# Two weight tiles of the dense mixture begin in the attention's wide score banks, one step before the fourth pair's values

## The chip, the cores and the metric

The kernel runs on one core of one Trainium2 chip. The metric is the device time of one execution in microseconds (us), the median of several runs. Engines are named as in the profile: PE is TensorE's matmul side and PEld its weight load, DVE is VectorE, ACT ScalarE, POOL GpSimd, and SP the engine whose queue issues the transfers.

## The reference, cut to what matters

Three stages follow one another. Only the first two meet at the place of the change.

```python
# 1. attention, B=4, H=8, S=576, D=64, block mask of 64
scores = where(block_i >= block_j, q @ k.T / sqrt(D), -1e9)
attn = softmax(scores);  x = (attn @ v)        # -> x: 2304 tokens x 512
# 2. dense mixture: w1, w2, w3 are 512 x 768, w_out is 768 x 512
h = maximum(maximum(x @ w1, x @ w2), x @ w3);  x = h @ w_out
# 3. four experts, weighted by normalised domain_probs
out = sum_e p[:, e] * (relu(x @ w1[e]) @ w2[e])
```

## The kernel before

**Attention by pairs of heads.** There are 16 pairs, `n` from 0 to 15, four to a batch. A turn of the main loop finishes pair `n` and starts pair `n + 1`. Its steps stand in a list, `todo`. `scores(n + 1, 0)`, `(…, 1)` and `(…, 2)` (steps s0, s1, s2) multiply q by k into PSUM (L181, L202), DVE takes the row minimum (L218), ACT the exponential (L225), and a later `normalise` multiplies by the reciprocal of the sum (POOL L251 from pair 4 on; for pairs 0 to 3 the output is scaled in `weigh` instead). `turn_probs` transposes probabilities on PE (L279), and ACT and DVE copy them out (L289): ta[0], ta[1] are the first part for either head, tb[0], tb[1] the second. `values(n)` (step va, L314) multiplies by v. For batch 0, `weigh` (transposes L337 and L341, products L342 and L345) scales the result. `prep_pair` (step pp) prepares the pair after the next.

**PSUM.** Eight banks: `ps_x` has four one-bank buffers (tag x) that scores, transposes and `weigh` take in turn. `ps_c` is one buffer of two banks (tag c), in which only step s2 of the first eight pairs puts part of its scores (and the last step of later pairs). `ps_v` has two banks for the values of batch 0. When batch 0's attention is over, `ps_v` is closed, and its banks become `ps_m`, two one-bank buffers for the mixture. From pair 4 on a run of scores begins only when all the buffers it needs are free (`whole`, with the ends kept in `x_ends` and `c_ends`).

**The mixture as filler.** `moe1(b)` is a generator for batch `b`: for each of six column tiles of h it multiplies three weight tiles (w1, w2, w3), each as 12 matmuls (four pairs' slices `d` of x, times the three terms high-high, high-low, low-high) of 128x128 by 128x512, L480, into one `ps_m` bank. ACT copies the first result to `mt` (L524), DVE takes the maximum with the others (L526). Then come four tiles of w_out. `Filler.upto` draws units of it between attention's steps of the next batch, by a pace: a turn's position `at` gives the units due, less `LAG` = 9. A weight tile of 12 matmuls counts three units. `moe1_inputs(b, ds)` splits the attention's output for pairs `ds` into a high and a low part (ACT L502, DVE L503). It is called for the first three pairs before the seventh step of a batch's last turn, and for the fourth pair after its values.

**Weights.** Before batch 0 uses a weight tile, `Convert` loads it and turns it into two float32 parts (ACT L399, L400, L94; POOL L405, L412; DVE L407, L408, L421), up to five tiles and two wide ones ahead.

**Order.** The program is traced in this order, and a scheduler then orders each engine's instructions by a timeline of its own: an instruction whose operands are ready and whose engine is free may go ahead of others that were traced earlier. On the chip each engine takes its instructions strictly in the order so fixed.

Of the kernel before, what the change touches and what calls it, by code (L numbers as in the profile page):

```python
# [6 lines left out]
F32 = mybir.dt.float32  # L7
# [5 lines left out]
ALU = mybir.AluOpType  # L13
# [8 lines left out]
P = 128  # L22
# [5 lines left out]
def program(tc, q, k, v, w123, w_out, probs, e_w1, e_w2, out):  # L28
    nc = tc.nc
# [5 lines left out]
    KD = DM // P  # L35
    NF = FF // P
    NPAIR = H // 2
# [5 lines left out]
    def f(ap):  # L43
        return ap.bitcast(F32)
# [26 lines left out]
    ps_c = attn.enter_context(tc.tile_pool(name="ps_c", bufs=1, space=PSUM, side="right"))  # L71
# [4 lines left out]
    mp = moe.enter_context(tc.tile_pool(name="moe", bufs=1))  # L76
    MAIN = 512
# [13 lines left out]
    pairs, later, made, exps, normal, least = {}, [], {}, [], [], []  # L91
# [48 lines left out]
    x_ends, c_ends = [], []  # L140
# [190 lines left out]
    def weigh(n, behind):  # L331

        pair = pairs[n]
        with tc.issue_after(behind.ins):
            rt = ps_x.tile([P, 512], F32, name="rt", tag="x")
            for m, i in enumerate((0, 2, 3, 1)):
                nc.tensor.transpose(  # L337
                    rt[:, P * i:P * (i + 1)], pair["rb"][:, m].rearrange("p h c -> p (h c)"), ident
                )
            r4 = pair["pv0"][:, P:2 * P]  # L340
            nc.tensor.transpose(r4, pair["rb4"], ident)  # L341
        x_ends.append([nc.vector.tensor_tensor(pair["xf"][:, 0:512], rt, pair["xf"][:, 0:512], op=ALU.mult)])  # L342
        for h in range(2):
            x = pair["xf"][own[h], 512:S]
            nc.vector.tensor_tensor(x, r4[own[h], 64 * h:64 * h + 64], x, op=ALU.mult)  # L345
# [12 lines left out]
    def weight_tile(n, wide):  # L358
        if wide:
            tag, bufs = "wo", 2  # L360
        else:
            tag, bufs = (("wt", 3), ("wu", WT - 3))[taken[0] % WT >= 3]
            taken[0] += 1
        return mp.tile([P, 2, tiles[n].shape[1], P], F32R, name=tag, tag=tag, bufs=bufs)
# [90 lines left out]
    def moe_weight(b, n):  # L455

        if b == 0:
            wt = convert.weight(n)
        else:
            A = tiles[n].shape[1]  # L460
            if b == B - 1 and n == 0:
                taken[0] = 0
            wide = n >= 3 * NF
            if b == B - 1 and not wide and n % WT >= 3:
                wide = True
                taken[0] += 1
            wt = weight_tile(n, wide)
            nc.sync.dma_start(out=f(wt[:].rearrange("p k a f -> p k (a f)")), in_=held[n][:, :, 0:A * P])
        return wt[:, 0], wt[:, 1]
# [5 lines left out]
    def mm3(out_, terms):  # L475
        n = 3 * len(terms)
        m = 0
        for wh, wl, xh, xl in terms:
            for w, x in ((wh, xh), (wh, xl), (wl, xh)):
                nc.tensor.matmul(out=out_, lhsT=w, rhs=x, start=m == 0, stop=m == n - 1)  # L480
                m += 1
                if m % 4 == 0 and m < n:
                    yield
# [3 lines left out]
    xs = {}  # L487

    def moe1_inputs(b, ds):
        if b not in xs:  # L490
            xs[b] = (
                mp.tile([P, KD, MAIN], F32R, name="xh", tag="xh"),
                mp.tile([P, KD, MAIN], F32R, name="xl", tag="xl"),
            )
        xh, xl = xs[b]
        for d in ds:
            xf = pairs[b * NPAIR + d]["xf"]
            rs = slice(b * REST, (b + 1) * REST)
            for cs, h, l in (
                (slice(0, MAIN), xh[:, d], xl[:, d]), (slice(MAIN, S), rest_x[0][:, d, rs], rest_x[1][:, d, rs]),  # L500
            ):
                nc.scalar.copy(h, xf[:, cs])  # L502
                nc.vector.tensor_tensor(l, xf[:, cs], f(h), op=ALU.subtract)  # L503

    def moe1(b):
        hidden = [mp.tile([P, NF, MAIN], F32R, name=x, tag=x) for x in ("hh", "hl")]
        whole = arena.rearrange("p (b d s) -> p d b s", b=B, d=KD)
        hs = [[x[:, ff] for ff in range(NF)] for x in hidden]
        runs = [(MAIN, "mt", *xs[b], *hs, lambda d: x2f[b][:, d, 0:MAIN])]
        if b == B - 1:  # L510
            room = [rest_h] + [mp.tile([P, 2, 2, B * REST], F32R, name="wu", tag="wu", bufs=2) for _ in range(2)]
            hs = [[x[:, i, j] for x in room for j in range(2)] for i in range(2)]
            runs.append((B * REST, "mr", *rest_x, *hs, lambda d: whole[:, d, :, MAIN:S]))
        for ff in range(NF):
            prev = [None] * len(runs)
            for n in range(3):
                wh, wl = moe_weight(b, 3 * ff + n)
                for c, (w, tag, xh, xl, hh, hl, _) in enumerate(runs):
                    m = ps_m.tile([P, 512], F32, name="m", tag="m")[:, 0:w]
                    yield from mm3(m, [(wh[:, d], wl[:, d], xh[:, d], xl[:, d]) for d in range(KD)])  # L520
                    t = prev[c]
                    if t is None:
                        t = prev[c] = mp.tile([P, w], F32, name=tag, tag=tag, bufs=2)
                        nc.scalar.copy(t, m)  # L524
                    else:
                        nc.vector.tensor_tensor(t, m, t, op=ALU.max)  # L526
                    if n == 2:
                        nc.gpsimd.tensor_scalar(hh[ff], t, 1.0, 0.0, op0=ALU.mult, op1=ALU.add)
                        nc.gpsimd.tensor_tensor(hl[ff], t, f(hh[ff]), op=ALU.subtract)
                    yield  # L530
        for d in range(KD):
            wh, wl = moe_weight(b, 3 * NF + d)
            for w, _, _, _, hh, hl, to in runs:
                m = ps_m.tile([P, 512], F32, name="m", tag="m")[:, 0:w]
                yield from mm3(m, [(wh[:, ff], wl[:, ff], hh[ff], hl[ff]) for ff in range(NF)])
                x = to(d)
                nc.scalar.copy(x, m if len(x.shape) == 2 else m.rearrange("p (b s) -> p b s", b=B))  # L537
                yield

    class Filler:  # L540
        def __init__(self):
# [15 lines left out]
    filler = Filler()  # L557

    def stage(fn, *args):
        old = later[:]  # L560
        later.clear()
        if fn is not None:
            fn(*args)
        for x in old:
            x()
# [16 lines left out]
    for n in range(NALL):  # L582
        b, d = divmod(n, NPAIR)
        ahead = n + 2 < NALL
        prep = prep_pair(n + 2) if ahead else iter(())
        g = 2 * n
        ta, tb = [[(turn_probs, g + h, part) for h in range(2)] for part in range(2)]
        va = (values, n)
        apart = n + 1 < 2 * NPAIR
        s0, s1, s2 = [(scores, n + 1, i) if n + 1 < NALL else (None,) for i in (0, 1 if apart else 3, 2)]  # L590
        pp = (next, prep, None)
        if apart:
            todo = [ta[0], s0, pp, tb[0], s1, ta[1], tb[1], s2, pp, va]
        else:
            todo = [ta[0], s0, pp, tb[0], ta[1], tb[1], s1, pp, va]
        for m, st in enumerate(todo):
            if d == NPAIR - 1 and m == 6:
                moe1_inputs(b, range(KD - 1))
            stage(*st)
            if b == 0 and m == 3 and n:  # L600
                weigh(n - 1, made["pv"])
            if d == NPAIR - 1 and m == len(todo) - 1:
                if b == 0:
                    weigh(n, made["pv"])
                moe1_inputs(b, [KD - 1])
            at = (n + (m + 1) / len(todo)) / NPAIR
            filler.upto((at - 1) * UNITS - LAG)
        if n + 4 < NALL:
            load_pair(n + 4)
        if d == NPAIR - 1:  # L610
            if b == 0:
                first.close()
                ps_m = ps.enter_context(tc.tile_pool(name="ps_m", bufs=2, space=PSUM, reuse_waits="tile"))
            filler.work.append(moe1(b))
# [26 lines left out]
    def tile_of(p, c, t):  # L641
        return (2 * p + c) * TPC + t

    pr = xp.tile([P, NTT, E], F32, name="pr", tag="pr")
    for p in range(NPASS):
        for c in range(2):
            if p < NPASS - 1:
                r0 = (2 * p + c) * S
                tc.keep_in_program_order(nc.sync.dma_start(
                    out=pr[:, tile_of(p, c, 0):tile_of(p, c, TPC)],  # L650
# [544 lines left out]
    for e in range(E):  # L1195
        for g in range(NG):
# [3 lines left out]
            for it in range(2):  # L1200
                n = 2 * g + it
                w = ready.pop(0) if ready else weights_in(e, n)
# [4 lines left out]
                made = next(following) if last else None  # L1207
# [7 lines left out]
            if begins:  # L1215
                tt_ = ps_o.tile([P, DM], F32, name="sh", tag="o")
                nc.tensor.transpose(tt_[0:E * NTT, 0:P], prt.rearrange("x e t -> x (e t)"), ident)
                t = temp()[:, 0:P]
# [14 lines left out]
    for p in range(1, NPASS):  # L1233
        es = list(range(E))[::-1] if p % 2 else list(range(E))
        background = mix() if p < NPASS - 1 else iter(())
        for m, e in enumerate(es):
# [4 lines left out]
            for n, i in enumerate(order):  # L1241
# [3 lines left out]
                w = kept_w.pop(0) if kept_w and m == 0 else weights_in(e, i)  # L1245
# [4 lines left out]
                made = next(following) if last else None  # L1250
# [82 lines left out]
```

## Time and profile before

| | |
|---|---|
| median of three runs | 1222.46 us (1220.34 to 1223.17) |
| the profiled execution | 1219.63 us |
| its span, first to last instruction | 1217.7 us |
| PE busy | 1190.4 us, 98% of the span |
| DVE, ACT, POOL busy | 833.7, 466.9, 295.6 us |
| mean granted TensorE clock | 0.993 |

The profile is of one execution; 1.93 us of its time lie outside the span. Times in the rows are counted from the span's start. In a timeline each line is a run of like instructions: start, length, engine, line of the program, operation, output <- input, count, and in brackets the time that the engine was idle before it and whose end released it.

### The profile page before, as it was taken

The page shows a single profiled execution, that of the slowest core. Times are in us where ns is not written, and L with a number is a line of the kernel's source. Part 1 is how long each engine was busy: PE and PEld are TensorE (multiplying, and loading weights), DVE is VectorE, ACT ScalarE, POOL GpSimd, SP SyncE. Part 2 cuts the span into 40 slices and gives each one's busy share as a digit, 9 for nine tenths or more (in the row PEclk, how much of TensorE's full clock was granted, in tenths as well). Part 3 has the DMA queues.
Part 4 walks back from the last instruction along what each step waited for, and adds up shares of the span by engine and source line. Part 5 has one row for each costly group of instructions (what it writes and reads, how often), then busy time and mean ns, then how long its engine had stood idle before and what let it go on. Part 6 is the DMA issues. An engine that isn't in the chain of part 4 may idle for free.

```text
span 1217.7 us, 18226 instructions
## 1 busy us (share of the span) xinstructions
PE 1190.4 (98%) x6941; PEld 1065.0 (87%) x6941; DVE 833.7 (68%) x1453; ACT 466.9 (38%) x974; POOL 295.6 (24%) x324
## 2 busy tenths in 40 slices
PE   7889999999999999999999999999999999999998
PEld 4567777778777888898999989999999999999998
DVE  4877874443445541778888895758697887587896
ACT  5976665454335111344434340232232213322222
POOL 2458853433421220433333340000000000000000
PEclk8999999999999999999999999999999999999999
DMA  5836765554423784878888865777887877676664
GB/s 205 274 130 221 247 213 173 164 150 146 139 87 106 272 293 136 302 272 317 319 297 311 303 207 198 282 284 279 344 309 297 322 295 277 233 272 234 250 214 176
DMA packets 82347, 290.67 MB, mean 239 GB/s; under 512 B 8716, under 2 KB 18004, under 8 KB 69204
## 3 DMA queue, kind: packets, MB, share of 16 engines
q1 hardware_dynamic: 82260, 289.51, 67.3%
q8 instruction: 55, 0.90, 0.3%
q14 instruction: 32, 0.26, 0.1%
HBM read 206.34 MB, written 83.14 MB: 238 GB/s over the span
## 4 chain that ended last, share of the span: by engine, by line
PE 80%; DVE 8%; DMA 5%; ACT 4%; issue 2%; POOL 1%; SPq 0%; DVEq 0%; ACTq 0%; POOLq 0%
PE m L844 23%; PE m L480 23%; PE o L1003 16%; PE pv L314 3%; PE tt L279 3%; PE st L181 3%; PE o L926 2%; PE o L930 2%; PE o L929 2%; PE m L1003 2%; DMA part<-in_e_w 2%; ACT p L225 1%; DMA t<-in_e_w 1%; PE st L202 1%; DMA w<-kb 1%
## 5 line engine op out<-in xcount | busy, mean ns | idle before, releaser
L844 PE MATMUL m<-t,w 128*128 128x384 f32 x1152 | 228.4, 336 | 0.0
L1003 PE MATMUL o<-hx,w 128*128 128x384 f32 x1176 | 226.1, 337 | 0.5 <-DMA w<-kb 0.4
L1003 PEld LDWEIGHTS o<-hx,w 128*128 128x128 f32 x1176 | 207.7, 188 | 1.1 <-PE m L844 0.7
L844 PEld LDWEIGHTS m<-t,w 128*128 128x128 f32 x1152 | 203.4, 188 | 2.7 <-DVE tmp L864 0.3
L844 PE MATMUL m<-b,w 128*128 128x384 f32 x864 | 175.5, 336 | 2.1 <-ACT tmp L869 2.1
L844 PEld LDWEIGHTS m<-b,w 128*128 128x128 f32 x864 | 153.1, 188 | 5.6 <-ACT tmp L869 2.4
L480 PE MATMUL m<-xh,wt 128*128 128x512 f32 x352 | 117.4, 396 | 0.0
L225 ACT ACTIVATE p<-st,mn 128x128 f32<-128x128 f32 (+2 forms) x144 | 78.6, 557 | 54.7 <-DVE mn L218 54.7
L864 DVE TENSOR_TENSOR tmp<-m,tmp 128x384 f32<-128x384 f32 x144 | 77.8, 549 | 21.0 <-PE m L844 18.5
L251 POOL TENSOR_SCALAR p<-p,sm 128x128 f32<-128x128 f32 (+4 forms) x108 | 72.0, 683 | 69.1 <-ACT high L119 34.0
L218 DVE TENSOR_REDUCE mn<-st 128x1 f32<-128x128 f32 (+2 forms) x144 | 67.9, 512 | 17.6 <-ACT p L225 9.9
L974 ACT CAST hx<-hq 128x768 fp32r<-128x768 f32 x49 | 40.7, 837 | 97.5 <-PE o L1003 74.2
L480 PEld LDWEIGHTS m<-xh,wt 128*128 128x128 f32 x352 | 65.6, 188 | 12.6 <-ACT arena L537 0.2
L926 PE MATMUL o<-w,hh 128*128 128x512 f32 x192 | 74.8, 392 | 0.5 <-ACT hh L904 0.5
L929 PE MATMUL o<-w,hh 128*128 128x512 f32 x192 | 74.8, 390 | 0.0
L930 PE MATMUL o<-w,hl 128*128 128x512 f32 x192 | 74.7, 391 | 0.0
L279 PE MATMUL tt<-ident,p 128*128 128x128 f32 x400 | 62.7, 286 | 11.2 <-ACT eh L289 6.9
L799 POOL TENSOR_TENSOR w<-part,w 128x512 fp32r<-128x512 f32 x32 | 49.5, 1568 | 92.9 <-ACT w L797 92.9
L279 PEld LDWEIGHTS tt<-ident,p 128*128 128x128 f32 x400 | 48.0, 146 | 25.1 <-ACT eh L289 8.3
L480 PE MATMUL m<-xl,wt 128*128 128x512 f32 x176 | 69.3, 394 | 0.0
L480 PE MATMUL m<-hh,wo 128*128 128x512 f32 x192 | 64.0, 400 | 0.9 <-ACT wo L94 0.9
L799 POOL TENSOR_TENSOR part<-mix,part 128x512 fp32r<-128x512 f32 x32 | 43.8, 1382 | 71.6 <-ACT part L797 65.8
(184 smaller groups left out, 2112.1 us busy)
## 6 DMA issues: line engine op xcount, KB each, us to landing
w<-kb SPq DMA_DIRECT2D x55, 1024.0 KB, 6.0
w<-ka SPq DMA_DIRECT2D x30, 1792.0 KB, 7.9
ka<-w SPq DMA_DIRECT2D x16, 1792.0 KB, 6.7
wt<-held SPq DMA_DIRECT2D x34, 512.0 KB, 4.1
kb<-part SPq DMA_DIRECT2D x16, 1024.0 KB, 6.9
kb<-w SPq DMA_DIRECT2D x16, 768.0 KB, 4.8
arena<-in_w SPq DMA_DIRECT2D x18, 512.0 KB, 4.7
wo<-held SPq DMA_DIRECT2D x12, 768.0 KB, 4.4
```

Source lines behind the costliest of these rows:

```text
L218: least.append(nc.vector.tensor_reduce(mn[:, m:m + 1], x, axis=AX.X, op=ALU.min))
L225: exps.append(nc.scalar.activation(to, x, ACTF.Exp, bias=mn[:, m:m + 1], scale=-1.0, accum_out=sm[:, m:m + 1],))
L251: normal.append(nc.gpsimd.tensor_scalar(x, x, sm[:, c:c + 1], 1.0, op0=ALU.mult, op1=ALU.mult))
L279: nc.tensor.transpose(tt[:, c:c + P], pt[i][:, k0:k0 + P], ident)
L480: nc.tensor.matmul(out=out_, lhsT=w, rhs=x, start=m == 0, stop=m == n - 1)
L799: eng.tensor_tensor(w[:, a:b, 1], raw[:, a:b], f(w[:, a:b, 0]), op=ALU.subtract)
L844: ins = nc.tensor.matmul(out=m, lhsT=a, rhs=b, start=start and n == 0, stop=stop and n == 3 * KH - 1, skip_group_check=True,)
L864: nc.vector.tensor_tensor(t, x, y, op=ALU.add)
L926: ins = nc.tensor.matmul(out=o, lhsT=hh[:, ts], rhs=wh, start=i == 0, stop=False)
L929: nc.tensor.matmul(out=o, lhsT=hh[:, ts], rhs=wl, start=False, stop=False)
L930: nc.tensor.matmul(out=o, lhsT=hl[:, ts], rhs=wh, start=False, stop=i == G - 1)
L1003: nc.tensor.matmul(out=o, lhsT=a, rhs=b, start=start and m == 0, stop=stop and m == 2, skip_group_check=True,)
```

## The change

In the turn of pair 3, the last of batch 0, step s2 (of pair 4) is taken from its place in the list, and a new step `begin` stands there. It takes the two-bank buffer of tag c and multiplies the first two weight tiles (w1 and w2 of the first column tile) by the first three pairs' slices: 18 matmuls, nine to a bank. After the values of pair 3, `weigh` and the split of its output, `go_on` adds the six matmuls of the fourth pair, ACT copies one bank out and DVE takes the maximum with the other. Then step s2 of pair 4 is run. `moe1(0)` starts its first column tile with the third weight tile, and the filler's count is raised by the six units that were done, so that the rest keeps its pace.

```diff
         for ff in range(NF):
             prev = [None] * len(runs)
-            for n in range(3):
+            if b == 0 and ff == 0:
+                prev = [made["begun"]]
+            for n in range(2 if prev[0] is not None else 0, 3):
...
+    def begin():
+        m = made["m"] = ps_c.tile([P, 1024], F32, name="m", tag="c")
+        begin_with(m, range(KD - 1))
+
+    def begin_with(m, ds):
+        xh, xl = xs[0]
+        for n in range(2):
+            wh, wl = moe_weight(0, n)
+            for d in ds:
+                for i, (w, x) in enumerate(((wh, xh), (wh, xl), (wl, xh))):
+                    nc.tensor.matmul(
+                        out=m[:, 512 * n:512 * n + MAIN], lhsT=w[:, d], rhs=x[:, d], start=d == 0 and i == 0,
+                        stop=d == KD - 1 and i == 2, skip_group_check=True,
+                    )
+
+    def go_on():
+        m = made["m"]
+        begin_with(m, [KD - 1])
+        t = made["begun"] = mp.tile([P, MAIN], F32, name="mt", tag="mt", bufs=2)
+        c_ends.append([
+            nc.scalar.copy(t, m[:, 0:MAIN]), nc.vector.tensor_tensor(t, m[:, 512:512 + MAIN], t, op=ALU.max),
+        ])
+        filler.done += 6
...
+        if n == NPAIR - 1:
+            todo = [ta[0], s0, pp, tb[0], s1, ta[1], tb[1], (begin,), pp, va]
...
                 moe1_inputs(b, [KD - 1])
+                if b == 0:
+                    go_on()
+                    stage(*s2)
```

## Rows read from the trace of the kernel before

**Rows 1.** The page: busy time by engine, and the granted clock in 40 slices.
```profile
PE 1190.4 (98%) x6941; PEld 1065.0 (87%) x6941; DVE 833.7 (68%) x1453; ACT 466.9 (38%) x974; POOL 295.6 (24%) x324
...
PEclk8999999999999999999999999999999999999999
```

**Rows 2.** Windows around the change: length, busy time (instructions) by engine, PEclk, DMA.
```profile
64.30:67.40 3.10, 0.02 (x1) 0.00 (x0) 2.39 (x8) 1.51 (x5) 2.01 (x3) 1.00 0.88 275
67.40:70.70 3.30, 2.82 (x14) 1.95 (x14) 1.04 (x3) 3.30 (x13) 0.19 (x1) 0.72 0.35 139
70.70:72.90 2.20, 2.20 (x11) 1.74 (x10) 2.12 (x4) 2.06 (x6) 2.20 (x4) 0.64 0.00 0
...
81.10:87.60 6.50, 6.50 (x37) 5.12 (x33) 3.45 (x10) 5.06 (x15) 2.56 (x4) 1.00 0.01 4
87.60:98.50 10.90, 10.90 (x64) 8.50 (x64) 9.42 (x16) 6.92 (x15) 8.56 (x9) 1.00 0.72 235
```

**Rows 3.** The timeline of PE, from the third pair's values to the mixture's first product.
```profile
59.27 0.87 PE L314 MATMUL pv<-eh,vraw 128*64 128x384 f32 x4
...
64.05 0.27 PE L341 MATMUL pv<-ident,arena 128*128 128x128 f32 x1
67.46 0.33 PE L279 MATMUL tt<-ident,p 128*128 128x128 f32 x1 [3.14 <-ACT eh L289]
...
70.68 2.23 PE L279 MATMUL tt<-ident,p 128*128 128x128 f32 x10
73.88 0.39 PE L181 MATMUL st<-high 64*128 64x256 f32 x2 [0.97 <-DVE low L124]
...
75.47 0.87 PE L314 MATMUL pv<-eh,vraw 128*64 128x384 f32 x4
...
79.93 0.33 PE L181 MATMUL st<-high 64*128 64x128 f32 x2
...
81.11 0.50 PE L480 MATMUL m<-xh,wt 128*128 128x512 f32 x1
```

**Rows 4.** The timelines of DVE and ACT in the same stretch.
```profile
55.00 0.68 DVE L503 TENSOR_TENSOR xl<-arena,xh 128x512 fp32r<-128x512 f32 x1
...
61.85 0.74 ACT L225 ACTIVATE p<-st,mn 128x576 f32<-128x576 f32 x1 [0.44 <-DVE mn L218]
...
66.48 0.66 ACT L400 ACTIVATE arena<-arena 128x512 int32<-128x512 uint32 x1 [1.59 <-POOL arena L412]
...
73.72 0.37 ACT L289 COPY eh<-tt 128x256 f32<-128x256 f32 x1
...
73.92 0.98 DVE L503 TENSOR_TENSOR xl<-arena,xh 128x512 fp32r<-128x512 f32 x1
...
76.04 0.47 ACT L225 ACTIVATE p<-st,mn 128x256 f32<-128x256 f32 x1
...
80.93 0.69 DVE L503 TENSOR_TENSOR xl<-arena,xh 128x512 fp32r<-128x512 f32 x1
```

**Rows 5.** The chain that ended last, one merged run of mixture products: start, length, count.
```profile
91.02 3.45 PE m L480 x15
```

**Rows 6.** The instructions on `mt` up to 110 us: nanoseconds, least, median, most.
```profile
L526 DVE TENSOR_TENSOR mt<-m,mt x4: 670/677/678, 88.8 to 107.6; 128x512 f32<-128x512 f32 x4
L524 ACT COPY mt<-m x2: 591/607/623, 86.3 to 95.7; 128x512 f32<-128x512 f32 x2
```

**Rows 7.** Timelines: POOL's normalising of s2 (pair 4), and PE's transposes that read it.
```profile
78.84 1.66 POOL L251 TENSOR_SCALAR p<-p,sm 128x256 f32<-128x256 f32 x3 [2.12 <-DVE sm L234]
...
83.73 0.82 PE L279 MATMUL tt<-ident,p 128*128 128x128 f32 x6
```

**Rows 8.** The timeline of PE at the end of batch 1's attention.
```profile
172.96 0.50 PE L480 MATMUL m<-hh,wo 128*128 128x512 f32 x1 [0.89 <-ACT wo L94]
...
185.25 0.87 PE L314 MATMUL pv<-eh,vraw 128*64 128x384 f32 x4
```

**Rows 9.** Windows of 20 us, the only one between 80 and 480 us with idle PE.
```profile
160.00:180.00 20.00, 17.95 (x91) 13.45 (x91) 15.56 (x28) 12.67 (x32) 12.15 (x14) 1.00 0.54 181
```

## The prediction

> **What bounds the kernel now.** I read the page first. PE is busy 98% of the span and its clock is below full mostly in the first fifteenth [rows 1]. Windows of 20 us then showed where PE still idles: before 80 us, in one stretch at 160 to 180 us [rows 9], and little in the rest of the mixture's filler phase. So early in the run time is lost by waiting, and from about 81 us on, where the mixture fills the gaps, each microsecond of PE work is a microsecond of the end.
>
> In the window of the change the timeline of PE shows two waits. After the third pair's outputs are scaled (the transpose at 64.05) PE idles 3.14 us until 67.46, and after the transposes at 70.68 it idles 0.97 us until step s2 at 73.88 [rows 3]. The first wait is ACT's: its queue stood 1.59 us for POOL's part of a weight conversion, and the copy that PE needed came behind that [rows 3, 4]. From 75.47 on there is no gap.
>
> Is PE truly full after 81 us, or only counted as busy? A run of 15 products of the mixture takes 3.45 us, 0.230 us each [rows 5], and in the stretch from 81.1 to 87.6 PE is busy 6.50 of 6.50 us at full clock [rows 2]. The Trainium skill (Trainium Kernel Development and Optimization, Performance Expectations) warns that matmul busy time is a bad measure, as matmuls are pipelined, and that the weight loads' busy share is better; it would speak against the change if there were hidden slack, since work taken out of a stretch with slack saves nothing. Here the weight loads are busy 5.12 of 6.50 us, 79% [rows 2]; I take the rest for pipeline, not slack, because products of 512 columns follow at an even 0.230 us [rows 5]. The sum keeps the full 0.230 us for each product moved.
>
> **The change, part by part.** The profiled execution took 1219.63 us with a span of 1217.7; the median is 1222.46, 2.83 above it. I add up differences and take them from the median.
>
> *Matmuls.* None is added or removed: 24 products go from behind 81 us to the turn of pair 3. Twelve of them (two tiles, first two pairs) need nothing late: the low half of the second pair's input is made at 55.00, and the two-bank buffer is free when the last exponential on it ends, at 61.85 + 0.74 = 62.59 [rows 4]. The two weight tiles are converted before that. The scheduler may send ready work ahead of work traced earlier, as it did with that input split, which is traced in this turn's seventh step and ran at 55 us. So I expect these twelve in the gap at 64.3: 12 x 0.230 = 2.76 us of work into 3.14 us of idling. **-2.76.** Bounds: 0, if the scheduler's timeline has no gap there and puts them behind the transposes, to -3.73, if the other gap of 0.97 us takes further products too.
>
> *The other twelve.* The six of the third pair need a low half that came at 73.92 + 0.98 = 74.90 [rows 4], and the six of the fourth pair come after the values. They move inside a stretch that PE fills anyway. **0**, hidden by nothing and saving nothing.
>
> *Step s2 leaves its place.* It held PE from 73.88 to 75.47, after the 0.97 us wait [rows 3]. Without it the values can start when the last copy they read is done, 73.72 + 0.37 = 74.09 [rows 4]: 1.38 us earlier. The 1.59 us of s2 are paid later. **+0.2.** Bounds: -1.0 (the 0.97 us saved whole) to +1.6 (the values start no earlier).
>
> *The clock.* After the wait of 3.1 us the granted clock is 0.72 for 3.30 us and 0.64 for 2.20 us [rows 2]: parts of these stretches ran at 1.2 instead of 2.4 GHz. What full clock would have done more is 3.30 x 0.28 + 2.20 x 0.36 = 1.7 us, if PE had never had to wait for ACT's copies and exponentials there. I take half, **-0.85**; bounds 0 and -1.7. The Trainium skill (TensorE: Matmul & The Clock Gate, Part 1) has idling lower the clock and activity release it; the rows agree with the fall after the gap. By that rule the whole 1.7 us could come back, which is the third rival below.
>
> *Evacuation.* One ACT copy (0.61 us) and one DVE maximum (0.68 us) [rows 6] as before, only earlier. **0.** Before, each had a full tile of other products to hide under; now s2 waits for both, as it needs the two-bank buffer.
>
> *What queues behind that wait.* Values start at 74.1 instead of 75.47, and the fourth pair's low half was done 6.15 us after they started (80.93 + 0.69 less 75.47) [rows 3, 4], so now at 80.2. Six products (1.4), copy and maximum (1.3) bring s2 to 82.9, against 73.88: nine microseconds late. Pair 5's step s0 takes the one-bank buffer that s2 uses, four places on in the ring, so it waits for s2's exponentials. They ended at 76.04 + 0.47, 2.6 us after s2's start [rows 3, 4], so s0 goes from 79.93 to 85.5: 5.6 us late. The transposes that read s2's output started at 83.73, and POOL finished that output at 78.84 + 1.66 = 80.50 [rows 7], 6.6 us after s2's start; that gives 89.5, 5.8 us late. In these 5 to 6 us PE has the first transposes of pair 4, the twelve late products, s2 itself and the third weight tile (2.76 us), and then further tiles that stand converted. So PE doesn't idle: **0**. If that cover failed, up to 5.6 us. Attention can catch up: without filler a turn took 75.47 - 59.27 = 16.2 us [rows 3], and batch 1's four took (185.25 - 75.47) / 4 = 27.4 us each [rows 3, 8].
>
> *Transfers.* `begin` draws the first two weights one turn's end earlier, so their loads and stores are traced ahead of the load of pair 7 on SP's queue. All of them had run long before, as the input halves and weights stood ready; **0**, and no gain.
>
> *Given back later.* Around 160 to 180 us PE idles 2.05 us [rows 9], the longest of it (0.89 us) for the conversion of an output weight tile [rows 8]. ACT, DVE and POOL work there behind one another, and PE will come there about 3 us sooner. Part of the conversions starts sooner too, since the first two weight buffers come free sooner. I give back **+0.6**; bounds 0 and +2.8 (all that was won in the first gap).
>
> Sum: -2.76 + 0.2 - 0.85 + 0.6 = -2.8 us, so 1222.46 - 2.8 = **1219.6 us** (1216.8 for an execution like the profiled one). About 0.2%, 2.4 us, is what a measurement of this kernel can tell from no change, and the forecast is just beyond it.
>
> **The rivals.**
>
> *Nothing is won (1222).* The products land where s2 stood, behind the wait of 3.14 us, or the stretch at 160 to 180 us takes everything back. The first would be so if the scheduler's own timeline doesn't see the gap, which came from a queue on ACT that ran late. For it: that gap is an accident of ACT's order [rows 4]. Against it: work that is ready goes ahead in this trace. By this way only the 0.97 us gap is filled, less some giving back: -0.5 us, 1222.0.
>
> *Slower (1226).* Pair 5's s0 starts 5.6 us late and attention doesn't catch up, as the filler that was drawn ahead leaves too little for the end of batch 1. The mixture of batch 1 can begin before its fourth pair's values only with 18 products (two banks, three pairs), 4.1 us. So the end moves by 5.6 us less what these cover: +1.5 to +5.6, middle +3.5, 1226.0. It decides once the fourth pair's values of batch 1 start later than 185.25. For it: DVE is busy 78% and POOL 61% of the window at 160 to 180 us [rows 9], so little room to catch up at the end. Against it: 27.4 us a turn against 16.2 us that a turn needs.
>
> *More than forecast (1217.5).* The clock never falls, both gaps are filled, nothing is given back: -3.73 + 0.2 - 1.7 = -5.2, some of it lost to the waits for ACT: -5, 1217.5. For it: the two low-clock windows stand right behind the gap [rows 2]. Against it: in them PE also waits for ACT's copies.
>
> **How the numbers follow.** Forecast 0.42, nothing won 0.28, slower 0.20, more 0.10. The forecast's own range is 1218 to 1221; about 0.31 of its 0.42 is beyond 0.2%. With the 0.10 that makes 0.41 for faster. Same: 0.11 from the forecast, 0.22 from the second case and 0.01 from the third, 0.34. Slower: 0.19 and 0.06, 0.25. The range reaches from 1217.2 (the better rival's gain of 5.2 us) to 1226.0 (the middle of the slower one): a tenth lies outside on the slow side, less on the other.
>
> **What would show it.** Right: in the timeline of PE some twelve products of 512 columns between the scaling transposes of pair 2 and the next wait, no gap of 3 us, a granted clock above 0.9 from 64 to 73 us, the values of pair 3 near 74 us, s2 of pair 4 near 83 us, and batch 1's last values about 2 us before 185.25. Wrong: the gap still there with 18 products behind it; PE idle between 80 and 90 us before s2 or s0; more than 2.05 us idle around 160 to 180 us, or batch 1's last values later than before, with the products of the mixture run out ahead of them.

## The result, and the profile after

The changed kernel took 1230.83 us (1227.26 to 1231.26, six runs), the kernel before 1221.34 beside it on the same chip (1217.87 to 1223.17, six runs). The ratio is 1.0085, with a 95% interval of 1.0069 to 1.0102: about 10 us slower. The prediction said 1219.6 and a range that ended at 1226.0. The profiled execution took 1231.26 us, with a span of 1229.2 us against 1217.7.

The page after, the rows that answer to [rows 1]:

```profile
PE 1196.3 (97%) x6941; PEld 1067.2 (87%) x6941; DVE 839.8 (68%) x1453; ACT 465.0 (38%) x974; POOL 292.5 (24%) x324
...
PEclk8999999999999999999999999999999999999999
```

The page shows almost nothing: the same 6941 matmuls, 5.9 us more of busy PE and 5.6 us more of idle PE. The stretches do. First the gap that the change was to fill, and the stretch of [rows 9]; these windows of after answer to [rows 2, 9] (length, busy time and instructions of PE, PEld, DVE, ACT, POOL, then PEclk and DMA):

```profile
64.50:68.00 3.50, 1.72 (x10) 1.13 (x8) 2.69 (x9) 1.91 (x5) 2.15 (x3) 1.00 0.87 282
68.00:72.00 4.00, 3.16 (x14) 1.89 (x14) 1.57 (x4) 4.00 (x14) 1.12 (x1) 0.77 0.22 90
72.00:75.40 3.40, 2.49 (x12) 1.94 (x11) 3.40 (x6) 1.81 (x6) 2.67 (x5) 0.77 0.38 104
160.00:180.00 20.00, 18.87 (x131) 13.03 (x130) 17.13 (x31) 15.47 (x41) 14.13 (x19) 1.00 0.60 193
```

The timeline of PE after, against [rows 3]; L552 is a product of `begin_with`, L480 one of the ordinary mixture:

```profile
64.58 0.48 PE L552 MATMUL m<-xh,wt 128*128 128x512 f32 x1
...
67.98 0.33 PE L279 MATMUL tt<-ident,p 128*128 128x128 f32 x1 [1.78 <-ACT eh L289]
...
75.43 0.86 PE L314 MATMUL pv<-eh,vraw 128*64 128x384 f32 x4 [0.50 <-ACT eh L289]
...
77.87 0.51 PE L552 MATMUL m<-xl,wt 128*128 128x512 f32 x1
...
80.63 0.44 PE L314 MATMUL pv<-eh,vraw 128*64 128x128 f32 x4
...
81.93 0.50 PE L480 MATMUL m<-xh,wt 128*128 128x512 f32 x1
...
86.19 0.39 PE L552 MATMUL m<-xh,wt 128*128 128x512 f32 x1
...
89.70 0.39 PE L181 MATMUL st<-high 64*128 64x256 f32 x2 [0.64 <-DVE mt L562]
```

Six of the 24 products ran in the gap, one more at 73.57, eleven at 77.87 to 80.63, in the middle of pair 3's values, and the last six, of the fourth pair, at 86.19, behind ordinary products of the next tiles that were put ahead of them at 81.93. Pair 3's values began at 75.43, not sooner than the 75.47 of [rows 3], and ended 2.8 us later for the cut. And s2 of pair 4, at 73.88 before [rows 3], starts at 89.70, 15.8 us later. The last thing that it waited for is the maximum on `mt`. Now the timelines of DVE, ACT and POOL after, in the same stretch, against [rows 4, 7]:

```profile
74.84 0.68 DVE L503 TENSOR_TENSOR xl<-arena,xh 128x512 fp32r<-128x512 f32 x1
...
82.00 0.69 DVE L342 TENSOR_TENSOR arena<-rt,arena 128x512 f32<-128x512 f32 x1 [5.54 <-PE pv L341]
...
83.37 0.69 DVE L503 TENSOR_TENSOR xl<-arena,xh 128x512 fp32r<-128x512 f32 x1 [0.33 <-ACT xh L502]
...
88.23 0.69 DVE L421 TENSOR_TENSOR wt<-arena,wt 128x512 fp32r<-128x512 f32 x1 [4.03 <-issue]
88.96 0.69 DVE L562 TENSOR_TENSOR mt<-m,mt 128x512 f32<-128x512 f32 x1
```

```profile
87.52 0.62 ACT L94 CAST wt<-arena 128x512 fp32r<-128x512 f32 x1 [4.03 <-PE m L552]
88.20 0.59 ACT L562 COPY mt<-m 128x512 f32<-128x512 f32 x1
```

```profile
89.96 0.76 POOL L405 TENSOR_SCALAR arena<-arena 128x512 f32<-128x512 f32 x1 [11.97 <-ACT arena L399]
...
98.01 1.67 POOL L251 TENSOR_SCALAR p<-p,sm 128x256 f32<-128x256 f32 x3 [1.48 <-DVE sm L234]
```

Read the brackets: DVE stands 5.54 us until pair 3's values are through and 4.03 us more before s2, ACT 4.03, POOL 11.97. PE is full of filler, but the three engines that attention and the weight conversion need are empty. ACT's 4.03 us are a wait for the last products at L552, as its next cast writes a weight buffer that they read. Before, that cast came at nearly the same time:

```profile
86.75 0.67 ACT L94 CAST wt<-arena 128x512 fp32r<-128x512 f32 x1
```

So the conversion goes on only 0.8 us later than before, and what the stretch lacks is attention's work, which stands behind s2. One window of 12 us says it, of before and of after:

```profile
78.00:90.00 12.00, 12.00 (x89) 9.66 (x86) 8.10 (x19) 8.42 (x23) 6.26 (x9) 1.00 0.14 35
```

```profile
78.00:90.00 12.00, 11.37 (x62) 8.77 (x64) 3.60 (x8) 3.72 (x8) 0.04 (x1) 1.00 0.09 27
```

DVE goes from 8.10 to 3.60 us of work, ACT from 8.42 to 3.72, POOL from 6.26 to 0.04. Does that come back later? The four turns of batch 1's attention (from one pair's values to the next, pairs 3 to 7) before, then after:

```profile
75.47:98.50 23.03, 23.03 (x164) 17.96 (x164) 16.33 (x34) 15.92 (x41) 14.03 (x17) 1.00 0.45 148
...
151.77:185.25 33.48, 31.43 (x187) 23.62 (x186) 25.13 (x50) 21.23 (x55) 18.14 (x22) 1.00 0.67 219
```

```profile
75.43:115.34 39.91, 39.27 (x239) 30.61 (x239) 25.66 (x47) 20.64 (x50) 21.59 (x25) 1.00 0.40 134
115.34:143.44 28.10, 27.26 (x180) 21.04 (x179) 22.70 (x37) 19.17 (x45) 23.17 (x24) 1.00 0.61 202
143.44:169.85 26.41, 24.41 (x159) 16.99 (x158) 21.70 (x36) 18.45 (x48) 18.19 (x23) 1.00 0.81 272
169.85:196.71 26.86, 24.06 (x150) 17.96 (x150) 17.20 (x41) 15.29 (x43) 13.21 (x16) 0.94 0.58 199
```

The first turn grows from 23.03 to 39.91 us. The same windows for the mixture's products at L480 alone (length, PE, PEld, PEclk, DMA) show what PE did in that time, in the first and the last turn before, then in the first, third and fourth after:

```profile
75.47:98.50 23.03, 14.09 (x55) 9.81 (x55) 1.00 0.45 148
...
151.77:185.25 33.48, 22.67 (x92) 16.47 (x91) 1.00 0.67 219
```

```profile
75.43:115.34 39.91, 25.13 (x99) 17.92 (x99) 1.00 0.40 134
...
143.44:169.85 26.41, 14.63 (x55) 9.38 (x54) 1.00 0.81 272
169.85:196.71 26.86, 15.28 (x54) 10.73 (x54) 0.94 0.58 199
```

PE used up 44 more ordinary products in the first turn and 17 at L552. They were missing at the end of the batch: the last turn had 54 instead of 92. Nor did attention catch up in the later turns: the third and the fourth, with 55 and 54 ordinary products, took 26.41 and 26.86 us, where before the first turn, with 55, took 23.03. DVE was busy 21.70 us of the third turn, but only 17.20 of the fourth, so how full DVE is doesn't explain the fourth by itself. So batch 1's last values start at 196.71 instead of 185.25, 11.5 us late, and the span is 11.5 us longer.

From 200 to 500 us PE is busy without a gap in both kernels, but for 0.33 us. What was not done by 200 us is therefore left at the end. Windows of before, then after:

```profile
80.00:200.00 120.00, 117.95 (x760) 91.42 (x761) 89.07 (x169) 80.09 (x201) 81.97 (x92) 1.00 0.63 206
...
500.00:1300.00 800.00, 710.54 (x3879) 684.61 (x3877) 565.00 (x881) 221.36 (x347) 87.56 (x60) 1.00 0.68 248
```

```profile
80.00:200.00 120.00, 113.40 (x727) 85.29 (x725) 87.97 (x159) 74.60 (x189) 75.22 (x85) 0.99 0.58 195
...
500.00:1300.00 800.00, 721.43 (x3933) 695.24 (x3931) 572.32 (x892) 226.57 (x357) 92.26 (x64) 1.00 0.68 250
```

54 more matmuls are left after 500 us, 721.43 - 710.54 = 10.9 us of PE. Idle PE from 80 to 200 us rises by 4.55 us only (120 less 113.40 against 120 less 117.95). The weight loads fall by more, 6.13 us. Part of the loss is thus time in which PE counts as busy and does less.

### The profile page after: what moved, and what is told of

The parts are those of the page before. It is cut to its first block, busy times and chain, and to the rows that moved or that the text cites. A ratio compares the mean times of both kernels' runs of the same rounds, so it can differ in the third digit from the quotient of the medians.

```text
span 1229.2 us, 18212 instructions
## 1 busy us (share of the span) xinstructions
PE 1196.3 (97%) x6941; PEld 1067.2 (87%) x6941; DVE 839.8 (68%) x1453; ACT 465.0 (38%) x974; POOL 292.5 (24%) x324
## 4 chain that ended last, share of the span: by engine, by line
PE 74%; DVE 8%; DMA 7%; ACT 5%; POOL 4%; issue 2%; SPq 0%; DVEq 0%; ACTq 0%; POOLq 0%
PE m L875 22%; PE m L480 20%; PE o L1034 17%; DMA t<-in_e_w 3%; PE tt L279 3%; PE pv L314 3%; PE st L181 2%; PE m L1034 2%; PE o L957 2%; PE o L961 2%; PE o L960 2%; ACT p L225 2%; DMA part<-in_e_w 2%; POOL arena L412 1%; DMA w<-kb 1%
## 5 line engine op out<-in xcount | busy, mean ns | idle before, releaser
L480 PE MATMUL m<-xh,wt 128*128 128x512 f32 x336 | 114.5, 401 | 0.8 <-DVE mt L528 0.8
L251 POOL TENSOR_SCALAR p<-p,sm 128x128 f32<-128x128 f32 (+4 forms) x108 | 68.2, 648 | 55.1 <-DVE sm L234 31.5
L480 PEld LDWEIGHTS m<-xh,wt 128*128 128x128 f32 x336 | 63.1, 190 | 13.7 <-DVE mt L528 1.2
L279 PEld LDWEIGHTS tt<-ident,p 128*128 128x128 f32 x400 | 48.6, 146 | 27.6 <-ACT eh L289 8.7
L528 DVE TENSOR_TENSOR mt<-m,mt 128x512 f32<-128x512 f32 x47 | 32.3, 687 | 52.0 <-PE m L480 50.0
L480 PE MATMUL m<-hh,wo 128*128 128x512 f32 x192 | 65.7, 405 | 2.1 <-ACT wo L94 1.7
L480 PE MATMUL m<-xl,wt 128*128 128x512 f32 x168 | 66.5, 396 | 0.0
```

Of the source, the lines that this page charges most:

```text
L251: normal.append(nc.gpsimd.tensor_scalar(x, x, sm[:, c:c + 1], 1.0, op0=ALU.mult, op1=ALU.mult))
L279: nc.tensor.transpose(tt[:, c:c + P], pt[i][:, k0:k0 + P], ident)
```

## The experiments

The theory: step s2 heads the next pair's attention, and its lateness stops ACT, DVE and POOL, whose work then can't be made up, as the weight conversion fills them. Where an expectation letters its theories, A is this one. The rivals are that the order of the new products behind other tiles, the cut into pair 3's values, or the early products themselves cost the time.

All runs in one table: how late s2 of pair 4 starts after pair 3's values (negative: ahead of them), when the values of pairs 4, 7 and 15 start (us, each kernel's own trace), and the ratio to the kernel before with its interval.

| run | s2 after values 3 | values 4 | values 7 | values 15 | ratio |
|---|---|---|---|---|---|
| before | -1.6 | 98.5 | 185.3 | 382.2 | 1 |
| changed | 14.3 | 115.3 | 196.7 | 391.6 | 1.0085 (1.0069 to 1.0102) |
| e1_only_s2_late | 3.6 | 103.7 | 181.9 | 384.1 | 1.0039 (1.0022 to 1.0057) |
| e11_s2_behind_one | 11.8 | 115.8 | 191.9 | 387.6 | 1.0057 (1.0040 to 1.0073) |
| e8_s2_behind_tiles | 14.0 | 113.6 | 192.6 | 388.3 | 1.0064 (1.0040 to 1.0089) |
| e12_none_early | 14.5 | 115.2 | 192.9 | 387.8 | 1.0056 (1.0036 to 1.0075) |
| e3_go_on_first | 15.8 | 115.6 | 197.1 | 392.0 | 1.0090 (1.0075 to 1.0105) |
| e4_values_whole | 15.5 | 116.0 | 197.7 | 392.5 | 1.0085 (1.0070 to 1.0100) |
| e2_s0_first | 17.7 | 120.9 | 195.9 | 390.7 | 1.0082 (1.0066 to 1.0098) |
| e5_parts_out | -2.0 | 102.6 | 192.2 | 388.3 | 1.0046 (1.0026 to 1.0067) |
| e9_s2_sooner | -5.6 | 99.6 | 186.3 | 383.2 | 1.0000 (0.9987 to 1.0014) |
| e6_before_no_second | -1.6 | 93.3 | 179.2 | 377.3 | 0.9962 (0.9947 to 0.9976) |
| e7_after_no_second | 14.1 | 110.5 | 182.7 | 378.5 | 0.9983 (0.9973 to 0.9994) |
| e10_parts_no_second | -2.8 | 97.9 | 183.1 | 380.1 | 0.9986 (0.9975 to 0.9997) |

**e1_only_s2_late.** The kernel before, with s2 of pair 4 put behind the last input split and nothing else changed:

```diff
+        if n == NPAIR - 1:
+            todo = [ta[0], s0, pp, tb[0], s1, ta[1], tb[1], pp, va]
...
                 moe1_inputs(b, [KD - 1])
+                if b == 0:
+                    stage(*s2)
```

> The kernel before, with one part of the change alone: step s2 of pair 4 is run behind the values of pair 3 instead of before them; no product is made early and the two-bank buffer stays free. Theory A (the late s2 holds up batch 1's attention, since the transposes of pair 4 and step s0 of pair 5 are traced behind it and share its ring of buffers): s2 no longer waits for products, only for the values, so it starts near 79 us instead of 73.9 (89.7 with the change); attention slips by about 5 us and the kernel is 2 to 5 us slower than before. Rival B (the loss comes from the early products themselves, which cut into the values and then hold the two-bank buffer): no product is early here, so within 1 us of before, s2 or not.

s2 came 3.6 us after the values, and the kernel took 1223.95 against 1219.20 us. A step of 1.6 us that is moved by 5.2 us (from 1.6 ahead of the values to 3.6 behind), without a product moved, costs 4.8 us. The prediction priced such a move at +0.2, and what queues behind it at 0. e1 too leaves more PE work behind 500 us than before, 713.59 against 710.54 us:

```profile
500.00:1300.00 800.00, 713.59 (x3890) 688.10 (x3888) 564.29 (x884) 222.54 (x349) 89.12 (x60) 1.00 0.67 249
```

**e3_go_on_first and e4_values_whole.** The changed kernel with the fourth pair's products, the copy and the maximum given priority over other tiles (e3), and with `begin` behind the values as well (e4):

```diff
-        begin_with(m, [KD - 1])
-        c_ends.append([...])
+        with tc.high_priority():
+            begin_with(m, [KD - 1])
+            c_ends.append([...])
...
-            todo = [ta[0], s0, pp, tb[0], s1, ta[1], tb[1], (begin,), pp, va]
+            todo = [ta[0], s0, pp, tb[0], s1, ta[1], tb[1], pp, va, (begin,)]    # e4 alone
```

> The changed kernel, with the fourth pair's six products and the copy and maximum behind them given high priority in the schedule, so that they run as soon as their input is there and not among the third and fourth tiles' products (in the trace of the change the input was ready at 84.1 us and these six ran from 86.2 to 88.2). Theory A: s2 starts some 3 us sooner, near 86 us, and the kernel gets back 2 to 3 of the 9.5 us. Rival B: the values are still cut in two by 14 products, so no change beyond 1 us.

> As the run with the six products first, and besides the eighteen early products are traced behind the values of pair 3 instead of before them, so that they fill gaps only and don't cut into the values. Theory A: values end near 78 instead of 81 us, s2 starts near 83 us, 6 to 7 us before the changed kernel's 89.7, and half or more of the loss of 9.5 us comes back: 1224 to 1227 us. Rival B in its first half (the cut alone is the loss): all comes back, 1221 or less. If the rival that the products were drawn too early and the filler runs out is right by itself, nothing comes back: 1230.

Neither moved s2: 89.93 and 90.37 us. The scheduler still put ordinary products ahead, as in e4's timeline of PE, where those of L552 stand among them at 86.85:

```profile
86.85 0.39 PE L552 MATMUL m<-xh,wt 128*128 128x512 f32 x1
...
90.37 0.39 PE L181 MATMUL st<-high 64*128 64x256 f32 x2 [0.63 <-DVE mt L563]
```

With s2 as late, the time was the same, 1.0090 and 1.0085. In e4 pair 3's values ran in one piece (seven of its products still ran ahead of them), so the cut alone isn't what costs. What an earlier `go_on` would be worth these two can't say.

**e2_s0_first.** The changed kernel with s2 of pair 4 moved into the next turn, behind step s0 of pair 5:

```diff
...
+        if n == NPAIR:
+            todo[2:2] = [(scores, n, 2)]
...
                     go_on()
-                    stage(*s2)
```

> The changed kernel, with step s2 of pair 4 traced in the next turn behind the first transposes of pair 4 and step s0 of pair 5, instead of ahead of both. The early products, their cut into the values and the late s2 itself all stay; only what stood behind s2 by the trace order alone goes ahead of it. Theory A (attention's lateness in batch 1 is the price, about 1 us for each us at first, 15 us late with the change): s0 of pair 5 starts 10 us or more earlier than 95.4, only the second transposes of pair 4 still wait for s2, and 3 us or more of the 9.5 come back: 1222 to 1227 us. The rival that early products are dear by themselves (the filler is drawn down): 1229 or more, as with the change.

s0 came 10 us sooner, at 85.11 instead of 95.35, s2 at 93.31, and the ratio stayed at 1.0082. The time, 1228.83 us, is the rival's (1229 or more) and not theory A's (1222 to 1227). So what the prediction thought would be late next, s0 behind s2 in the ring of buffers, isn't what costs. Pair 4's own values came 27.6 us behind s2, 5.6 us later than in the changed kernel, and that cost nothing more either: their start doesn't set the time by itself.

**e8_s2_behind_tiles and e11_s2_behind_one.** The kernel before, with no new product at all; s2 of pair 4 waits for the ordinary mixture's first maximum, two tiles in (e8), or for its first copy, one tile in (e11):

```diff
+        if n == NPAIR - 1:
+            todo = [ta[0], s0, pp, tb[0], s1, ta[1], tb[1], pp, va]
+        if n == NPAIR:
+            filler.upto(6)                      # e11: 3
+            c_ends.append([made["max"]])        # the maximum of L526; e11: the copy of L524
+            stage(scores, n, 2)
```

> The kernel before without any early product: the first two weight tiles are made in the mixture's own banks as before, but step s2 of pair 4 is traced behind them and waits for the maximum that ends them, as it does with the change. Theory A: s2 starts near 88 us, attention is as late as with the change, and the kernel is as slow: 8 to 11 us above before. The rival that the early products or the held two-bank buffer carry the loss: within 5 us of before, since s2 alone, behind the values, cost 4.8.

> As the run with s2 behind the first two weight tiles, but behind the first alone (it waits for ACT's copy of that tile): a dose between the late s2 by itself (76.6 us, 4.8 us lost) and behind both tiles (86.3 us, about 8 us lost). If each microsecond that s2 is late costs in proportion: s2 near 82 us, 6 to 7 us slower than before. If the loss is a step that any disturbance of this turn's order brings: 4 to 5 us, like the smallest dose.

Both are slower, 1.0064 and 1.0057, some 7.8 and 6.9 us, though they contain nothing of the change but the wait, and the units of the first tiles drawn ahead of it. By the medians the cost grows less than the lateness: 4.8 us at 3.6 us behind the values, 6.9 at 11.8, 7.8 at 14.0. The intervals are wide (2.7 to 6.9 us for e1, 4.9 to 10.8 for e8), so the shape of this growth is not shown.

**e6_before_no_second and e7_after_no_second.** Both kernels without the middle of the weight conversion (the instructions of its `second()` on POOL and DVE are left out; the matmuls stay):

```diff
     # second():
-            a = self.buf(i, "a")
-            nc.gpsimd.tensor_scalar(a, a, MOST, LEAST, op0=ALU.min, op1=ALU.max)
...
-            nc.gpsimd.tensor_tensor(ai, ai, self.buf(i, "r").bitcast(I32), op=ALU.add)
+            pass
```

> The kernel before with the middle part of the weight conversion left out (two POOL and two DVE operations for each of 26 pieces; the weights of batch 0's mixture and what follows from them come out wrong). It is the base for the next run. In the trace this part takes about 1.9 us of POOL and 1.1 us of DVE a piece. If PE bounds batch 1 as the prediction had it: no change beyond 2 us. If attention and the conversion share the bound on ACT, DVE and POOL there: 2 to 6 us faster than before.

> The changed kernel with the same part of the conversion left out (same wrong weights). Theory A with the conversion as the reason why attention does not catch up: the turns of pairs 5 to 7 become shorter than 26 us, and the distance to the run without the change and without this part falls from 9.5 to 4 us or less. If attention's own chain of steps is what can't catch up, or the early products cost by themselves: the distance stays at 8 us or more.

The kernel before becomes 4.6 us faster by it (1213.82 against 1218.44), so PE alone did not bound batch 1. The two without it stand 0.21% apart, 1216.26 against 1213.82 us, instead of 0.85%. The long turn is still there in e7, and the next two take 27.90 and 27.41 us, full of ordinary products (80 and 78); the last one is short. Windows of the first and the last turn, then of the last turn's ordinary products alone (L471 in this kernel):

```profile
70.09:110.53 40.44, 39.86 (x242) 31.31 (x242) 20.05 (x42) 24.96 (x60) 15.14 (x18) 1.00 0.58 208
165.84:182.72 16.88, 14.82 (x120) 11.65 (x119) 9.06 (x26) 9.48 (x28) 5.46 (x8) 1.00 0.28 92
```

```profile
165.84:182.72 16.88, 6.04 (x25) 4.36 (x24) 1.00 0.28 92
```

16.88 us is near the turn without filler that the prediction had counted on (16.2), but this turn has 25 ordinary products where the changed kernel's last has 54. At 0.230 us each the 29 fewer are 6.7 of the 10.0 us between the two turns, so the short turn alone proves little. The distance between the kernels does: s2 is as late in e7 (14.1 us), and without the middle of the conversion three quarters of the loss come back. Whether that is the time which the conversion takes from POOL and DVE or the length of its own chain, these runs don't separate.

**e5_parts_out and e10_parts_no_second.** The changed kernel with s2 back at its place: `begin` multiplies twelve products (two pairs) as early as in the gap, ACT and DVE copy the two parts out, and the rest is added later. e10 leaves out `second()` as well.

```diff
...
+            todo = [ta[0], s0, pp, tb[0], (begin,), s1, ta[1], tb[1], s2, pp, va]
...
+        begin_with(m, range(2))
+        made["parts"] = [mp.tile([P, MAIN], F32, name="mt", tag="mt", bufs=2) for _ in range(2)]
+        c_ends.append([nc.scalar.copy(made["parts"][0], m[:, 0:MAIN]),
+                       nc.vector.tensor_copy(made["parts"][1], m[:, 512:512 + MAIN])])
+        filler.done += 2
```

> The early products without the late s2: twelve products (two tiles, first two pairs) go into the two-bank buffer right behind the first transposes that finish pair 3's first head, both banks are copied to SBUF at once (one ACT, one DVE copy), and s2 stands where it stood before. The later products of the two tiles are added to the copies by DVE (two additions and a maximum where there were a copy and a maximum). Theory A: s2 near 74 us, attention as before, no loss; the gain is the filled gap of 3.1 us less the added copies, 0 to 3 us faster than before (1218.5 to 1221.5). If early products cost by drawing the filler down, it is slower than before by 2 us or more.

> The run whose twelve early products leave the banks at once and whose s2 stands in place, with the middle of the weight conversion left out (same wrong weights as in the two runs without it). To be read against the kernel before without that part, 1213.8 us. If the gap's filling was worthless because batch 1 is bound by attention and conversion together, it should now bring something, since PE is nearer to being the bound: 1 to 3 us faster, 1211 to 1213. If a filled gap is worth nothing because the steps that follow it wait for ACT and DVE anyway, and the added copies delay them: 0 to 4 us slower, 1214 to 1218.

Here the gap is filled as the prediction wanted it: 3.00 of 3.40 us, a wait of 0.43 us left. e5's windows, and the rows of its PE timeline that end the gap and come next:

```profile
64.30:67.70 3.40, 3.00 (x15) 2.18 (x13) 2.65 (x8) 1.81 (x5) 2.15 (x3) 1.00 0.93 297
67.70:71.60 3.90, 3.01 (x13) 1.80 (x13) 1.40 (x4) 3.90 (x13) 0.97 (x3) 0.82 0.18 74
71.60:75.90 4.30, 2.46 (x12) 1.77 (x10) 4.02 (x8) 3.12 (x9) 2.88 (x3) 0.77 0.21 58
75.90:80.00 4.10, 4.08 (x28) 2.97 (x30) 1.94 (x5) 1.29 (x5) 1.36 (x2) 0.63 0.23 91
```

```profile
67.74 0.33 PE L279 MATMUL tt<-ident,p 128*128 128x128 f32 x1 [0.43 <-ACT eh L289]
...
75.92 0.39 PE L181 MATMUL st<-high 64*128 64x256 f32 x2 [1.18 <-ACT p L225]
...
77.89 1.55 PE L314 MATMUL pv<-eh,vraw 128*64 128x384 f32 x4
```

The transposes at 67.74 come when ACT's copy comes, as before; s2 starts 2.0 us and the values 2.4 us later than in [rows 3]. 1224.33 us, 1.0046: slower, and without the middle of the conversion too: 0.9986 against e6's 0.9962, some 2.9 us. Filling the gap did not pay even with s2 in place, which is the second case of e5's expectation. DVE has three operations of 128x512 more here (a copy and two additions, 1456 instructions against 1453), and ACT's copy stands earlier; their part of the price wasn't measured apart.

**e9_s2_sooner.** The kernel before with s2 of pair 4 ahead of ta[1]:

```diff
+        if n == NPAIR - 1:
+            todo = [ta[0], s0, pp, tb[0], s1, s2, ta[1], tb[1], pp, va]
```

> The kernel before, with step s2 of pair 4 moved the other way in the same turn: ahead of the transposes of pair 3's second head instead of behind them (step s1 stands right before it). Theory: the values of pair 4 follow s2 by 24 to 28 us in every run so far, so a sooner s2 makes batch 1's attention sooner. s2 near 71 instead of 73.9 us, the values of pair 3 about as before, those of pair 4 1 to 3 us sooner, the kernel 0.5 to 3 us faster than before. If only lateness costs and batch 1 is bound by something else once s2 is on time: within 1 us of before.

s2 at 70.92, and 1.0000 (0.9987 to 1.0014). The gain of 0.5 to 3 us that the theory expected did not come: an s2 that is sooner than before is worth nothing.

**e12_none_early.** The changed kernel with all 24 products behind pair 3's values, s2 still behind their maximum:

```diff
-        begin_with(m, range(KD - 1))
+        with tc.issue_after(made["pv"].ins):
+            begin_with(m, range(KD - 1))
...
-            todo = [ta[0], s0, pp, tb[0], s1, ta[1], tb[1], (begin,), pp, va]
+            todo = [ta[0], s0, pp, tb[0], s1, ta[1], tb[1], pp, va]
...
                     moe1_inputs(b, [KD - 1])
+                    begin()
                     go_on()
```

> The eighteen products of the first two tiles are put behind the values of pair 3, so none runs in the gap at 64 us and none cuts those values; step s2 of pair 4 still stands behind the two tiles' maximum. Theory (only the lateness of s2 counts): s2 starts at 89 to 91 us, batch 1's last values at 196 to 198, and the time is 1229 to 1231 us, 8 to 11 above before, as with the whole change. Rival (the early products and the cut that they make into pair 3's values carry a part of it themselves): pair 3's values end near 78 instead of 81, s2 comes by 86 to 87 us, and the time is 1225 to 1227 us, 5 to 7.5 above before.

Each side was half right. s2 stood at 88.91, as the theory had it, but the time was the rival's: 1226.63 us, 1.0056, the value of e8 and e11. e12's timeline of PE:

```profile
67.62 0.47 PE L279 MATMUL tt<-ident,p 128*128 128x128 f32 x1 [3.16 <-ACT eh L289]
...
74.42 0.87 PE L314 MATMUL pv<-eh,vraw 128*64 128x384 f32 x4 [1.10 <-ACT eh L289]
...
77.83 0.48 PE L553 MATMUL m<-xh,wt 128*128 128x512 f32 x1
...
88.91 0.39 PE L181 MATMUL st<-high 64*128 64x256 f32 x2
```

The gap of 3.16 us is back, and the kernel is, by the ratios, some 3.5 us faster than the changed one. The three runs with a late s2 and no early product lie at 1.0056 to 1.0064, the four with both at 1.0082 to 1.0090. Single intervals still touch (1.0075 and 1.0069). So of the 10 us, about 7 are the late s2, and about 3 seem to come with the early products. Where these 3 us arise stays open: e12's turns differ from the changed kernel's in the third and fourth most (25.24 and 24.76 us instead of 26.41 and 26.86), and no run takes that apart. The granted clock of the fourth turn, 0.94 in the changed kernel and 1.00 in e12, doesn't sort the runs: e8 has 0.94 as well, and e2 has 1.00.

## Why the prediction was wrong, point by point

The failed step is *What queues behind that wait*, and in it the price of 0. It saw that s2 would be nine microseconds late and followed the lateness to PE alone: to s0, to the transposes, to filler that covers them. Three things were off.

- The size. It expected s2 at 82.9 us. The values began no earlier, were cut for 2.8 us, and the last six products waited behind other tiles: 89.70.
- The bearer. The prediction asked whether PE idles between 80 and 90 us, and PE hardly does. ACT, DVE and POOL do, and filler on PE covers none of their work. e8 and e11 show that the wait by itself costs some 7 us.
- "Attention can catch up", from a turn of 16.2 us. That turn is pair 3's, ahead of batch 1. In batch 1's turns the conversion stands between the scores and the transposes on the same engines, and a turn with 54 products took 26.86 us. e6 and e7 show the cause: with s2 as late, but without the middle of the conversion, the loss fell to 2.4 us.

The *slower* rival had this mechanism and its point of decision, with a chance of 0.20: batch 1's last values did come after 185.25, at 196.71. Its size was too small, as it took 5.6 us less up to 4.1 us for 18 products that would cover it; measured were 11.5 us at that point. e1, where those values come at 181.9 and the kernel is slower all the same, shows that the point doesn't decide alone: its next turn took 29.60 us, where before's took 24.35. The PE work that is left after 500 us goes with the time better: 3.05 us more than before in e1, 10.9 us in the changed kernel.

*Matmuls* (-2.76): six products in the gap instead of twelve, and nothing won, as values began at 75.43. The products ran in the order in which `begin_with` traces them, so the second tile's six, which needed nothing late, stood behind the third pair's three of the first tile, whose low half was made at 74.84. e5 traces the twelve alone and has all of them in the gap; with the gap filled nothing was won either. The transposes behind the gap wait for ACT, so a filled gap brings only what PE does in it, 1.4 us for six products here, and that was lost in the later waits. *The clock* (-0.85): 0.77 and 0.77 after the gap against 0.72 and 0.64 [rows 2]; no gain can be seen in the starts that follow. *Step s2 leaves its place* (+0.2): the values still waited 0.50 us for a copy, and the later payment was not 1.59 us of s2 but the chain. *Transfers*, *Evacuation* and *The other twelve* (0 each): in themselves nothing against them. The copy at 88.20 starts as the last product ends (87.78 + 0.39), and copy and maximum together take until 89.65, 1.45 us where the prediction had 1.3. *Given back later* (+0.6): the place was wrong. PE idles less than before at 160 to 180 us, 1.13 us against 2.05 [rows 9]; the longest waits came after, in this timeline of PE after, against [rows 8]:

```profile
181.08 0.66 PE L279 MATMUL tt<-ident,p 128*128 128x128 f32 x4 [1.16 <-POOL p L251]
...
183.01 0.79 PE L480 MATMUL m<-hh,wo 128*128 128x512 f32 x1 [1.28 <-ACT wo L94]
```

What made PE look full was a number that the prediction had and explained away. It took weight loads of 79% for a full PE and applied that to all of batch 1. The turn of pair 7 before shows 23.62 of 33.48 us, 71%, and after 17.96 of 26.86, 67%, with PE named busy 94% and 90%. The Trainium skill (Trainium Kernel Development and Optimization, Performance Expectations) calls the weight loads' share the better measure, and the runs agree: from 80 to 200 us busy PE fell by 4.55 us and the weight loads by 6.13 us, while 10.9 us more of PE work was left at the end.

## What to carry to other kernels

Before a step is moved, ask which engines work for it and stand still until it comes: filler on PE hides a late step from PE, and from nobody else. A turn's shortest time is read from a turn with the same work on the other engines, not from one ahead of it; look at how full DVE, ACT and POOL are there. And a gap that ends with another engine's copy is worth at most the work put in it, less what that work displaces; the first step of a chain behind it (here s2: 1.6 us long, 4.8 us dearer when moved by 5.2 us) can cost more than the gap held.

## What the runs showed of the hardware that was not expected

Filling the gap raised the clock in no way that can be seen. With PE busy 3.00 of 3.40 us in it (e5), the granted clock read 0.82, 0.77 and 0.63 in the next three windows, the last of them with PE busy 4.08 of 4.10 us; parts of each ran at 1.2 instead of 2.4 GHz. With the gap empty it read 0.72 and 0.64 [rows 2]. Over the stretch from 60 to 80 us it doesn't go by the filling either: with the gap empty it read 0.91 (before, e1), 0.83 (e9, e12) and 0.74 (e8, e11), with products in it 0.91 (the changed kernel), 0.84 (e5), 0.82 (e3), 0.75 (e2) and 0.74 (e4), each in one execution. The Trainium skill (TensorE: Matmul & The Clock Gate, Part 1) has idling lower the clock; here it was low also behind a gap that was filled, in stretches where PE waited for ACT in short pieces, and no run separates the two.
